# Block-sparse attention ahead of an FFN: scores in eight 64x32 tiles, probabilities turned by VectorE, block-diagonal values, sampled blocks copied on chip

## The chip, the cores and the metric

One core of a Trainium2 chip runs the whole program. Its engines are TensorE (PE; its weight loads are listed apart as PEld), VectorE (DVE), ScalarE (ACT), GpSimd (POOL) and SyncE (SP, which here only issues DMAs). Each engine works through its own instructions in order. The metric is the device time of one execution in microseconds (us); lower is better.

## The reference

Attention over a sparse set of key blocks, then a feed-forward net with an exact GELU. There are 4 batches, 8 heads, 768 positions and 64 dimensions per head. Positions form 24 blocks of 32. A query block sees its own block and both neighbours, the first and the last block, and three sampled blocks; the first and the last query block see all 24.

```python
scores = scale * np.matmul(q, k.transpose(0, 1, 3, 2))
mask = np.abs(blk_i - blk_j) <= window
mask = mask | (blk_i == 0) | (blk_j == 0) | (blk_i == n_blocks - 1) | (blk_j == n_blocks - 1)
for qb in range(n_blocks):
    for kb in sampled_blocks[qb]:
        mask[qb * block:(qb + 1) * block, kb * block:(kb + 1) * block] = True
scores = np.where(mask, scores, -1000000000.0)
scores = scores - np.max(scores, axis=-1, keepdims=True)
attn = np.exp(scores)
attn = attn / (np.sum(attn, axis=-1, keepdims=True) + 1e-09)
out = np.matmul(attn, v)
...
x = out.transpose(0, 2, 1, 3).reshape(B * S, H * D)      # 3072 x 512
h = x @ w_in                                             # 512 -> 2048
g = 0.5 * h * (1.0 + erf(h * inv_sqrt2))
return g @ w_out                                         # 2048 -> 512
```

A sampled block may repeat or coincide with a neighbour, the first or the last block; it must then count once.

## The kernel before

The work is cut into eight **units**: a batch and a half of its query blocks (12 blocks, 384 positions). A unit has an attention part and an FFN part. The main loop (L511) puts the FFN of one unit next to the attention of the next: first the eight steps of FFN1 (`ffn1_step`, L409), then `attention` (L432) of the next unit, into which the pieces of FFN2 (`ffn2_pieces`, L417; four matmuls each) are dealt as filler, one a round, to keep PE busy.

**Preparation.** Keys and queries come from HBM by DMA from POOL's queue, cast to bf16, with six consecutive positions in a partition. `prep_pair` (L187) turns a pair of heads on PE into the PSUM tile `pt` (two buffers of psT); DVE copies it to `kT` (L203), ACT scales it into `qT` (L205). For batches 1 to 3 this lies between the FFN1 steps of the second unit of the batch before.

**Attention by rounds.** A unit has two dense rounds (its one dense block, four heads each) and six sparse rounds (two query blocks each, the last one). A round has five stages:

- `stage_scores` (L296): 4 heads in 32-row strips; each query block meets its three neighbours straight from `kT` (96 columns) and 160 columns from `kg`, where the first, three sampled and the last key blocks stand side by side. Two row halves of PE (heads are paired in 64 partitions) and four column strips are used, so that the four products of a group stand in four tiles. DVE takes the row maxima (L319, one instruction per query block).
- `stage_exp` (L331): four ACT exponentials of 256 columns with the maximum as bias.
- `stage_transpose` (L342): PE turns the probabilities, 128x128 at a time, into PSUM tile `tp`; ACT copies it to `ps` (L351), every fourth time DVE (L353).
- `stage_av` (L356): products with the values, 65 columns (64 and a column of ones that gives the sum), from `vg0` (neighbours and first block) and `vg1` (sampled and last); then DVE adds 1e-9, takes the reciprocal and multiplies (L378 to L385).
- `stage_x` (L391): PE turns the outputs, DVE copies them into `xT` (L405), the input of FFN1.

`attention` runs these stages as a pipeline: in step `it` the scores of round it+1, the values of it-1, the transposes of it, the exponentials of it+1, the outputs of it-2, then one piece of FFN2.

**Gathers.** Sampled keys are copied on chip, with the block number in a register (`k_sampled`, L216, on DVE and POOL). Values go through a scratch copy in HBM (`v_scratch`, L223): each sampled block is fetched from there with its own DMA (`v_sampled`, L228, 33 a unit, on SP's and POOL's queues), the neighbours in larger ones (`v_fetch`, L252), and for batch 0 in part by DVE copies (`v_adjacent`, L233). `value_list` (L152) replaces a block number that would count twice by that of a block of zeros.

**Buffers.** psA (scores and FFN1 results) and psT have two buffers, psO (FFN2) and psV (value products) one each. In the head, the first score round runs after two pairs of heads are prepared.

## Time and profile before

| what | us |
|---|---|
| time, median of 3 runs | 362.96 |
| the three runs | 361.33, 362.96, 363.54 |
| span of the profiled execution (the page gives no other time for it) | 361.4 |
| first FFN1 step of the first unit starts | 52.0 |
| FFN1 of units 2, 4, 6 and 8 starts | 96.7, 181.1, 259.1, 334.9 |
| last FFN1, FFN2 and stores, to the end | 26.5 |
| busy: PE / PEld / DVE / ACT / POOL | 304.6 / 174.8 / 199.4 / 221.2 / 106.3 |

The groups of instructions that the change touches, of the whole run (busy time of the group; mean of one instruction):

| group | count | busy us | mean ns |
|---|---|---|---|
| PE score products, sparse (L301, two forms) | 1408 | 28.4 and 27.7 | 240 and 213 |
| PE transposes of probabilities (L347) | 448 | 46.9 | 233 |
| PE value products (L372, sparse) | 1408 | 25.4 | 203 |
| ACT exponentials of 256 columns (L337) | 176 | 69.6 | 480 |
| ACT copies of turned probabilities (L351) | 50 | 46.8 | 935 |
| DVE maxima of 512 columns (L319) | 88 | 57.1 | 686 |
| DVE copies of sampled keys (L220) | 149 | 20.0 | 224 |
| POOL copies of sampled keys (L220) | 115 | 27.7 | 299 |
| value DMAs from scratch, 32.5 KB each | 270 | | 4.3 to 5.0 us to landing |

How to read it: the busy time of a group is the time in which at least one of its instructions ran, and the mean is the length of one; where neighbours overlap, the mean is longer than the distance from one to the next. In the 40 slices of the span PE's clock is granted in full except in slices 4 to 6 (about 27 to 54 us), where it is halved. A busy PE is not a PE at its peak. What a stage costs is seen in the table by stretches of time and in the timeline, from where one start stands to the next.

### The profile page before, as it was taken

Reading aid. Unit: us, or ns where it says so; the run is one execution under the profiler, and the core shown is the slowest. Engines: PE = TensorE matmul, PEld = TensorE weight load, DVE = VectorE, ACT = ScalarE, POOL = GpSimd, SP = SyncE. Lnnn points to the kernel's source line nnn. Section 1 sums busy time; section 2 is a strip of 40 time slices with the busy share of each in tenths; the row PEclk is TensorE's granted clock in tenths of the full one; section 3 lists DMA queues with packets and bytes.
Section 4 is the critical chain, followed back from the end, with each engine's and each line's share of the span. In section 5 each row is a group of like instructions: output and inputs, shape, how many; then the busy total and the mean of one; then the engine's idle time right before and its main releaser. Section 6 shows DMA issues by size and latency. Waiting matters only on the chain.

```text
span 361.4 us, 13108 instructions
## 1 busy us (share of the span) xinstructions
PE 304.6 (84%) x5143; PEld 174.8 (48%) x5200; DVE 199.4 (55%) x606; ACT 221.2 (61%) x362; POOL 106.3 (29%) x248
## 2 busy tenths in 40 slices
PE   0852779958999979993999989998999999999994
PEld 0532545435554545452555555555554555455541
DVE  5598953698564854174546675157564862286000
ACT  1342754657658874683458875687558776786721
POOL 8393508600055505562302003863200310000000
PEclk9995558999999999998799999999999999999999
DMA  8988997992288999969377754959470630000001
GB/s 115 120 203 181 160 206 141 212 149 64 80 190 183 151 259 139 217 158 215 70 160 95 153 126 73 133 139 213 102 163 3 149 74 31 2 33 32 29 31 59
DMA packets 67328, 45.29 MB, mean 125 GB/s; under 512 B 30625, under 2 KB 61922, under 8 KB 67266
## 3 DMA queue, kind: packets, MB, share of 16 engines
q0 software_dynamic: 39104, 16.24, 38.1%
q1 hardware_dynamic: 28162, 28.21, 31.7%
q8 instruction: 41, 0.67, 0.8%
q14 instruction: 21, 0.17, 0.2%
HBM read 47.03 MB, written 9.62 MB: 157 GB/s over the span
## 4 chain that ended last, share of the span: by engine, by line
PE 53%; ACT 17%; DVE 14%; issue 9%; DMA 3%; POOL 2%; DVEq 0%; POOLq 0%; ACTq 0%
PE hp L413 25%; PE op L422 11%; ACT pp L337 9%; PE tp L347 6%; DVE nm L319 5%; PE sc L301 4%; PE av L372 4%; PE pt L193 4%; DVE vg L240 3%; ACT ps L351 3%; DVE nm L327 2%; DMA vg<-vscr 2%; ACT L339 2%; ACT pp L339 2%; POOL kg L220 1%
## 5 line engine op out<-in xcount | busy, mean ns | idle before, releaser
L413 PE MATMUL hp<-xT,w_in_sb 128*128 128x384 bf16 x512 | 90.5, 330 | 2.5 <-DVE xT L405 2.5
L422 PE MATMUL op<-w_out_sb,g 128*128 128x512 bf16 x327 | 85.6, 381 | 5.4 <-ACT os L427 1.4
L337 ACT ACTIVATE pp<-sc,nm 128x256 bf16<-128x256 f32 x176 | 69.6, 480 | 12.1 <-DVE den L378 7.2
L415 ACT ACTIVATE g<-hp 128x768 bf16<-128x768 f32 x64 | 51.9, 810 | 38.1 <-PE hp L413 38.0
L319 DVE TENSOR_REDUCE nm<-sc 128x2 f32<-128x512 f32 x88 | 57.1, 686 | 27.0 <-PE sc L301 19.1
L351 ACT COPY ps<-tp 128x1024 bf16<-128x1024 bf16 (+2 forms) x50 | 46.8, 935 | 38.6 <-PE tp L347 37.7
L413 PEld LDWEIGHTS <-w_in_sb 128*128 128x128 bf16 x512 | 48.5, 99 | 35.5 <-issue 5.0
L230 POOL DMA_DIRECT2D vg<-vscr x78 | 39.1, 503 | 78.6 <-DMA vscr<-vn 41.8
L422 PEld LDWEIGHTS <-g 128*128 128x128 bf16 x384 | 34.9, 98 | 34.2 <-issue 5.3
L347 PE MATMUL tp<-identity,pp 128*128 128x128 bf16 x448 | 46.9, 233 | 4.8 <-ACT pp L339 1.9
L327 DVE TENSOR_REDUCE nm<-sc 128x1 f32<-128x768 f32 x16 | 15.3, 958 | 53.7 <-PE sc L301 53.7
L372 PE MATMUL av<-vg,ps 128*32 128x65 bf16 x1408 | 25.4, 203 | 21.2 <-issue 7.8
L220 POOL COPY kg<-kT 128x128 bf16 x115 | 27.7, 299 | 50.6 <-PE sc L301 29.7
L372 PEld LDWEIGHTS <-ps 128*32 128x32 bf16 x1792 | 22.5, 99 | 37.0 <-issue 10.5
L301 PE MATMUL sc<-kT,qT 64*32 64x96 bf16 (+2 forms) x832 | 37.7, 234 | 3.1 <-issue 3.0
L301 PEld LDWEIGHTS <-qT 64*32 64x32 bf16 x1536 | 23.8, 96 | 33.3 <-issue 31.7
L347 PEld LDWEIGHTS <-pp 128*128 128x128 bf16 x448 | 27.5, 102 | 19.6 <-ACT pp L337 9.5
L109 POOL DMA_DIRECT2D vn<-in_v_dram x24 | 21.1, 916 | 42.7 <-DVE kg L220 41.9
L427 ACT COPY os<-op 128x512 f32<-128x512 f32 x24 | 14.2, 593 | 30.3 <-PE op L422 30.3
L301 PE MATMUL sc<-kg,qT 64*32 64x160 bf16 x704 | 28.4, 240 | 4.2 <-DVE kg L220 3.9
L203 DVE COPY kT<-pt 128x768 bf16<-128x768 bf16 x16 | 15.3, 957 | 16.0 <-PE pt L193 16.0
L385 DVE TENSOR_TENSOR xh<-av,rec 128x256 bf16<-128x256 f32 (+1 forms) x64 | 22.9, 358 | 2.2
(50 smaller groups left out, 228.8 us busy)
## 6 DMA issues: line engine op xcount, KB each, us to landing
vg<-vscr SPq DMA_DIRECT2D x192, 32.5 KB, 4.3
out_dram<-os SPq DMA_DIRECT2D x24, 256.0 KB, 2.1
vg<-vscr SPq DMA_DIRECT2D x6, 682.5 KB, 8.5
vscr<-vn SPq DMA_DIRECT2D x4, 780.0 KB, 4.1
kn<-in_k_dram POOLq DMA_DIRECT2D x8, 384.0 KB, 6.4
vn<-in_v_dram POOLq DMA_DIRECT2D x24, 128.0 KB, 7.2
vg<-vscr POOLq DMA_DIRECT2D x78, 32.5 KB, 5.0
vg<-vscr SPq DMA_DIRECT2D x6, 390.0 KB, 4.9
```

The lines of the kernel that those rows point to most:

```text
L220: copy(kg[:, (j - 1) % US, :, BL + BL * r:2 * BL + BL * r], kTs[b % 2][:, :, bass.ds(vals[j, r] * BL, BL)])
L230: engine.dma_start(out=vg1s[(j - 1) // US][BL * r:BL * r + BL, (j - 1) % US, :], in_=vscr[b][bass.ds(val * BL, BL), :])
L301: nc.tensor.matmul(out_, lhsT=qT[rows, h // 2, j * BL:(j + 1) * BL], rhs=rhs[rows], start=True, stop=True)
L319: nc.vector.tensor_reduce(out=nm[:, 2 * i:2 * i + 2], in_=A4[:, i], op=ALU.max, axis=AX.X, negate=True)
L337: nc.scalar.activation(pp[:, cols], A[:, cols], AF.Exp, bias=nm[:, i:i + 1])
L347: nc.tensor.transpose(T[:, c, :], pp[:, c * P:(c + 1) * P], identity)
L351: nc.scalar.copy(ps[:, 0:n, :], T[:, 0:n, :])
L372: nc.tensor.matmul(av[32 * hh:32 * hh + 32, s, :], lhsT=probs[:, 32 * hh:32 * hh + 32], rhs=vals[:, VW * h:VW * h + VW], start=(c == 0), s ...
L385: nc.vector.tensor_tensor(xh[:, at:at + n, :], av[:, 0:n, 0:D], rec[:, 0:n, None].to_broadcast([P, n, D]), op=ALU.mult)
L413: nc.tensor.matmul(hp[:, i, 0:UT], lhsT=w_in_sb[:, ki, (m + i) * P:(m + i + 1) * P], rhs=xT[:, ki, :], start=(ki == 0), stop=(ki == KIN - 1))
L415: nc.scalar.activation(g[:, m:m + 2, :], hp[:, :, 0:UT], AF.Gelu)
L422: nc.tensor.matmul(op, lhsT=g[:, m, t * P:(t + 1) * P], rhs=w_out_sb[:, m, :], start=(m == 0), stop=(m == KOUT - 1))
```

## The change

The units, the FFN and their interleaving stay. What changes:

- **Layout.** One tile `kvs[i]` holds, per key block, 128 columns of keys (four pairs of heads) and 2 x 130 columns of values. Values are block-diagonal: partitions 32hh to 32hh+31 hold 32 keys of head hh (of four), and heads 0 and 1 of a pair of strips have separate 65 columns, with zeros in the other's. The value DMAs (one a head, eight a batch) write there in place; `value_frame` writes the zeros and ones once. A 25th block has zero values and the keys of block 0. The scratch copy in HBM and all DMAs from it are gone.
- **Gathers.** For each query block three whole key and value blocks of 388 columns are copied on chip into `gbs`, with the block number (of `value_list`) in a register: 15 a batch by DVE, 51 by POOL, after the fourth FFN1 step of the batch before. In the head keys (128 columns) and values (260) are copied apart, as the keys of batch 0 lie in another tile, `k0`.
- **Scores.** Heads of the second group of four stand in the other row half, so that eight products (four heads, two groups) fall on eight 64x32 tiles. A query block has 24 products of 96, 64 and 96 columns instead of 16 of 96 and 160. One DVE instruction takes the maxima of a round.
- **Probabilities.** ACT writes the exponentials with the columns of two neighbouring key blocks interleaved, so that a pair of bf16 values fills a 4-byte word; one DVE instruction then turns all 32x32 blocks of words. The PE transposes and their copies are gone.
- **Values.** For two rounds (four query blocks) together: 64 rows (two heads' keys), 32 queries, 130 columns; eight tiles; 32 products a query block instead of 16. Division by DVE and output transposes once per two rounds; ACT copies to `xT` (two of them now).
- **Rounds.** Both dense blocks are in a batch's first unit: ten rounds there, six in the second. FFN2 pieces are single matmuls, 4 or 6 a round. psT has one buffer, psV is twice as large.
- **The head.** All eight preparations come first, then all ten rounds, without filler, then value copies on DVE, then all value products. Keys and queries are loaded whole, eight positions in a partition.

The diff, cut to its core:

```diff
+    V2 = 2 * VW
+    KC = NPR * BL
+    BW = KC + 2 * V2
+    PI = 8
+    PP = S // PI
...
+    kvs = [const.tile([P, NB + 1, BW], BF16, name=f"kv{i}") for i in range(2)]
+    gbs = [const.tile([P, US, NR, BW], BF16, name=f"gb{i}") for i in range(2)]
+    qT0 = const.tile([P, NPR, S], BF16, name="qT0")
+    qT1 = const.tile([P, (NB + 1) * KC], BF16, name="qT1")
+    qTs = [qT0, qT1[:, 0:NPR * S].rearrange("p (r s) -> p r s", r=NPR)]
+    k0 = qT1.rearrange("p (n c) -> p n c", c=KC)
+    kn = const.tile([P, H, PI * D], BF16, name="kn")
+    qn = const.tile([P, H, PI * D], BF16, name="qn")
+    ptd = const.tile([P, 2, NE, 2, BL, 2], BF16, name="ptd")
+    xTs = [const.tile([P, KIN, UT], BF16, name=f"xT{i}") for i in range(2)]
...
+    def load_v(b, h):
+        G, hh = divmod(h, 4)
+        c0 = KC + V2 * G + VW * (hh % 2)
+        nc.gpsimd.dma_start(out=kvs[b % 2][32 * hh:32 * hh + 32, 0:NB, c0:c0 + D],
+                            in_=v[b, h].rearrange("(n p) d -> p n d", p=BL))
...
+    def value_frame(i, engine):
+        kv = kvs[i]
+        engine.memset(kv[:, :, KC:BW], 0.0)
+        for hh in range(4):
+            c0 = KC + VW * (hh % 2) + D
+            engine.memset(kv[32 * hh:32 * hh + 32, 0:NB, c0:c0 + V2 + 1:V2], 1.0)
+
+    value_frame(0, nc.vector)
+    for h in range(H):
+        load_v(0, h)
...
+    def prep(b, which, pr, on_act):
+        src = kn if which == "k" else qn
+        pt = psT.tile([P, PI, PP], BF16, name="pt", tag="T")
+        for i in range(PI):
+                r = h2 ^ (pr // 2)
+                nc.tensor.transpose(pt[64 * r:64 * r + 64, i, :],
+                                    src[0:PP, 2 * pr + h2, i * D:(i + 1) * D],
+                                    identity[0:PP, 0:PP])
+            dst = keys(b)[:, 0:NB, BL * pr:BL * pr + BL].rearrange("q n (a i) -> q n a i", i=PI)
+            seen = pt.rearrange("q i (n a) -> q n a i", n=NB)
...
+    def gather(b, js, vals, engine, src=None, c0=0, c1=BW):
+        src = kvs[b % 2][:, :, c0:c1] if src is None else src
+            gb = gbs[(j - 1) // US]
+                engine.tensor_copy(gb[:, (j - 1) % US, r:r + 1, c0:c1],
+                                   src[:, bass.ds(vals[j, r], 1), :])
...
+    def rounds_of(hf):
+        js = list(range(j0, j0 + US))
+        dense = [("d", x, G) for x in (0, 1) for G in (0, 1)] if hf == 0 else []
+        return dense + [("s", tuple(js[i:i + 2])) for i in range(0, US, 2)]
...
+        def product(o, G, hh, j, rhs):
+            r = (hh % 2) ^ G
+            rows = slice(64 * r, 64 * r + 64)
+            pr = 2 * G + hh // 2
+            nc.tensor.matmul(o, lhsT=qT[rows, pr, BL * j:BL * j + BL],
+                             rhs=rhs[rows, :, BL * pr:BL * pr + BL], start=True, stop=True)
+        if rnd[0] == "s":
+            A4 = A.rearrange("p (g j c) -> p g j c", g=2, j=2)
+            for i, j in enumerate(rnd[1]):
+                gb = gbs[(j - 1) // US]
+                for c0, c1, rhs in ((0, 96, kT[:, j - 1:j + 2, :]),
+                                    (96, 160, kT[:, 0:NB:NB - 1, :]),
+                                    (160, 256, gb[:, (j - 1) % US, :, :])):
+                        for G in range(2):
+                            product(A4[32 * hh:32 * hh + 32, G, i, c0:c1], G, hh, j, rhs)
...
+            nc.vector.tensor_reduce(out=nm[:, 0:2 * n].rearrange("p (g j) -> p g j", g=2),
+                                    in_=A4[:, :, 0:n, :], op=ALU.max, axis=AX.X, negate=True)
...
+        def one(dst, src, bias):
+            nc.scalar.activation(dst.rearrange("p (c k e) -> p c e k", e=2, k=BL),
+                                 src.rearrange("p (c e k) -> p c e k", e=2, k=BL),
+                                 AF.Exp, bias=bias)
...
-        T = psT.tile([P, 8, P], BF16, name="tp", tag="T")
-        n = 4 * (len(grp) - 1) if grp[0] == "sparse" else NT
-        for c in range(n):
-            nc.tensor.transpose(T[:, c, :], pp[:, c * P:(c + 1) * P], identity)
-            nc.scalar.copy(ps[:, 0:n, :], T[:, 0:n, :])
-            nc.vector.tensor_copy(ps[:, 0:n, :], T[:, 0:n, :])
...
+    def turned(rnd):
+        pp = st.pop((rnd, "pp"))
+        if rnd[0] == "s":
+            w = 512 * len(rnd[1])
+            pt = ptpool.tile([P, 1024], BF16, name="pT")
+            nc.vector.transpose(pt[:, 0:w].bitcast(F32), pp[:, 0:w].bitcast(F32))
...
+            slots = [(rnd, i, j) for rnd in grp for i, j in enumerate(rnd[1])]
+            for G in range(2):
+                c0 = KC + V2 * G
+                for c in range(8):
+                    for s, (rnd, i, j) in enumerate(slots):
+                        x = len(rnd[1]) * G + i
+                        pv = st[rnd, "pt"][:, 256 * x:256 * x + 256]
+                        pv = pv.rearrange("p (c k e) -> p c k e", k=BL, e=2)
+                        if c < 3:
+                            src = kv[:, j - 1 + c, c0:c0 + V2]
+                        elif c < 5:
+                            blk = (0, NB - 1)[c - 3]
+                            blk = NB if abs(blk - j) <= 1 else blk
+                            src = kv[:, blk, c0:c0 + V2]
+                        else:
+                            src = gbs[hf][:, (j - 1) % US, c - 5, c0:c0 + V2]
+                        for h in range(2):
+                            rows = slice(64 * h, 64 * h + 64)
+                            nc.tensor.matmul(av[32 * s:32 * s + 32, h, V2 * G:V2 * G + V2],
+                                             lhsT=pv[rows, c // 2, :, c % 2], rhs=src[rows],
+                                             start=(c == 0), stop=(c == 7))
...
+            nc.scalar.copy(xTs[hf][:, :, t0:t0 + 32 * n], T[:, :, 0:32 * n])
...
+    def attention(b, hf, filler):
+        rounds = rounds_of(hf)
+        n = len(rounds)
+        ends = grouped(rounds, hf)
+        late = 12
+        per = -(-(KOUT * (UT // P) - late) // (n + 1))
+
+        def fill(m):
+            for _ in range(m):
+                next(filler, None)
         for it in range(-1, n + 2):
+            if it + 1 < n:
+                scores(b, rounds[it + 1])
             if 0 <= it - 1 < n:
+                turned(rounds[it - 1])
+            if it + 1 < n:
+                maxima(rounds[it + 1])
             if 0 <= it < n:
+                exponentials(rounds[it])
+            fill(per // 2 if it <= n - 1 else late // 4)
+            if it - 2 in ends:
+                outputs(hf, ends[it - 2])
+            if it - 1 in ends:
+                values(b, hf, ends[it - 1])
+                divided(ends[it - 1])
+            fill(per - per // 2 if it <= n - 1 else late // 4)
...
+        fetch()
+        groups = list(grouped(rounds, 0).values())
+        for i, grp in enumerate(groups):
+            values(0, 0, grp)
+            divided(grp)
+            if i:
+                outputs(0, groups[i - 1])
+        outputs(0, groups[-1])
...
+    for pr in range(NPR):
+        prep(0, "k", pr, False)
+    for pr in range(NPR):
+        prep(0, "q", pr, True)
+    spare_key(0, nc.vector)
+    gather_keys(J0[5:], v_pool0, nc.gpsimd)
+    gather_keys(J0[:5], v_dve, nc.vector)
+    for part in range(4):
+        load_w_in(part)
+    for part in range(2):
+    gather_values(J0[5:], v_pool0, nc.gpsimd)
+    gather_keys(J1, v_pool1, nc.gpsimd)
+    gather_values(J1, v_pool1, nc.gpsimd)
+    value_frame(1, nc.gpsimd)
+    first_attention(lambda: gather_values(J0[:5], v_dve, nc.vector))
...
+            if fresh:
+                prep(b + 1, "k" if s < 4 else "q", s % 4, s >= 4)
+                if s == 3:
+                    spare_key(b + 1, nc.vector)
+                    gather(b + 1, J0[:5], v_dve, nc.vector)
+                    gather(b + 1, J0[5:], v_pool0, nc.gpsimd)
+                    gather(b + 1, J1, v_pool1, nc.gpsimd)
```

509 lines of the change are left out of this document (160 added, 349 removed).

## The prediction

> **What bounds the kernel now.** I read the busy table by stage first. It was asked for from the second FFN1 step (batch 0, second half) on, two units with their FFN to a line; the next such step starts the next line:
>
> ```profile
> 96.60:181.00 84.40, 73.50 (x1272) 42.14 (x1288) 43.41 (x144) 55.03 (x91) 35.57 (x76) 0.96 0.90 176
> 181.00:259.00 78.00, 72.02 (x1272) 41.33 (x1288) 43.88 (x144) 54.97 (x91) 24.51 (x54) 1.00 0.76 135
> 259.00:334.80 75.80, 72.42 (x1272) 40.97 (x1288) 42.91 (x143) 54.91 (x91) 5.54 (x22) 1.00 0.25 61
> ```
>
> The columns are the stretch and its length, busy time of PE, weight loads, DVE, ACT and POOL, clock, DMA share and GB/s. The work is the same three times. PE is the bound at 72 to 73 us; the first two batches are 8.6 and 2.2 us longer than the third, with more DMA and hardly more PE work. The busy table of the last attention alone (310.0 to 334.7) has PE 23.2, ACT 18.6 and DVE 16.2 of 24.7 us. There the timeline shows ACT and PE in turn:
>
> ```profile
> 319.04 1.01 ACT L351 COPY ps<-tp 128x1024 bf16<-128x1024 bf16 x1 [0.38 <-PE tp L347]
> 319.95 1.57 ACT L337 ACTIVATE pp<-sc,nm 128x256 bf16<-128x256 f32 x4
> 320.35 0.43 PE L372 MATMUL av<-vg,ps 128*32 128x65 bf16 x32
> 320.72 1.14 PE L347 MATMUL tp<-identity,pp 128*128 128x128 bf16 x8
> 321.95 1.57 ACT L337 ACTIVATE pp<-sc,nm 128x256 bf16<-128x256 f32 x4 [0.43 <-PE tx L402]
> ```
>
> The transposes wait for the exponentials, and their 1.01 us copy out of PSUM stands on ACT between two rounds' exponentials: 2.6 us of ACT a round, in rounds of 2.5 to 3.1. The chain of waits holds one larger gap, in the middle of the value products:
>
> ```profile
> 166.04 0.35 PE av L372 x29
> 166.39 5.16 issue
> 171.55 0.25 PE av L372 x3
> ```
>
> What it waited for the profile doesn't name; it lies where sampled values come in by DMA.
>
> **The change, part by part.** First the loop, in the last batch's undisturbed times.
>
> *Removed.* A batch loses 112 PE transposes (56 ns start to start, 6.3 us, and waits of 0.2 to 0.3 us between pairs), 11.7 us of ACT copies (L351: 46.8 / 4), most of its value DMAs and POOL's issues of them.
>
> *Added on DVE.* Transposing 128x512 words has no row. Nearest are a 128x1024 bf16 copy out of PSUM at 0.68 and two 128x512 reduces at 1.29; I take 0.65 (ends 0.45 and 1.2: 3 us less, 10 us more over the kernel). One reduce of 1024 replaces two: 1.25, between 0.69 and 1.29. The division for two rounds is 0.16 + 0.18 + about 0.7 (128x256 took 0.42). The xT copies move to ACT, 0.59 each (row of 128x512, L351). A pair round then costs DVE 1.9 and half of 1.1, ACT 1.58 + 0.3 + 0.25 (os): both under 2.5. Exponentials written in interleaved pairs keep their 0.395 (upper end 0.59, L427's 512 columns: 9 us more in all).
>
> *PE.* Matmul starts in the records stand 3 to 4 ns apart inside a four of different tiles, and a four with 65 columns follows the last after 27 ns; eight tiles are therefore 54 ns, by issue and, at 130 columns, by streaming alike. So I take 0.06 us for eight value products (0.24 a block; now 0.19) and 0.15 a block for 24 scores (now 0.23). Where the shape of tiles changes, the next start comes 0.1 us late (scores to values 160 ns against 60, FFN2 to scores 309 against 216). The unit with six rounds, on PE: FFN2 48 x 0.216 = 10.4, scores 1.7, values 2.6, 12 output transposes 0.7, 27 changes of shape 2.7: 18.1. I took the instructions of PE, DVE and ACT in their order through these durations, each starting when its engine and its inputs are ready: PE waits 0.9 and 1.9 for os (one psO buffer, and os stands behind exponentials), 0.6 for the last division, and 0.9 pass until the last xT copy: 22.4. The unit with both dense blocks has 1.3 of dense scores and 1.5 of dense values more, 22.4 on PE, and waits of 4.4, the longest 1.0 for the last division, 0.7 for a transpose: 26.8. The same walk gives the old attention 28.5 where the trace has 24.7, as it lets a consumer start on whole tiles only; I take 1 us off each for that: **21.5 and 25.8**. FFN1 stays 10.9, and 15.4 with the preparations (8 pairs of 96 columns for 6 of 128). Their one psT buffer hides behind the 1.9 us steps: 0.96 copy, 0.6 transposes; without that cover, 0.5 for each of 8.
>
> *The gathers.* Between FFN1's fourth step and the attention DVE copies 15 blocks of 388 columns and POOL 51. POOL's 128 columns go every 0.24 us, and a 128-column memset took 0.12 more than a 1-column one; I take 0.5 for 388 (ends 0.24 and 0.72). Alone, DVE copied 11 blocks of 128 columns in 1.43; beside POOL's copies 6 took 2.98:
>
> ```profile
> 17.94 5.06 POOL L220 COPY kg<-kT 128x128 bf16 x21
> ...
> 19.83 2.98 DVE L220 COPY kg<-kT 128x128 bf16 x6
> ...
> 53.64 1.43 DVE L220 COPY kg<-kT 128x128 bf16 x11
> ```
>
> The first of the six lasted 1.83, the others came every 0.23, one to a POOL copy, and POOL's pace stayed. So here 15 x 0.5 = 7.5, from 8.8 after FFN1's start to 16.3, and the first maximum, due at 16.0, waits. PE has 2.5 us of queued scores and FFN2 as cover. I charge 0.7. [...]
>
> A batch is 25.8 + 21.5 + 10.9 + 15.4 + 0.7 = **74.3**, 1.5 under the clean 75.8; the larger gain is the 8.6 + 2.2 of the disturbed ones, as value DMAs leave the loop.
>
> *The head.* FFN1 starts at 52.0 now. The change (a) puts a 25x260 bf16 memset on DVE ahead of the block list: 3,250 words by 260 in 0.275 is 3.4 us, so the first kT copy comes at 11, not 9.1; (b) prepares all keys and queries through one psT buffer before any score: four times 0.96 + 1.05 + 0.1 and four times 0.81 + 1.05 + 0.1, so scores start at 27 (now 11.3); loads of 1.57 MB at the 121 GB/s of the first 10 us are in by 15; (c) runs ten rounds with DVE the bound: 1.9 to fill, 4 x 1.46, 5.5 x 1.9, ending at 45; (d) queues 15 value copies on DVE behind them and ahead of every division, beside a busy POOL: 6, ends 3 and 10; (e) then three groups of 2.0 (halved clock, as 27 to 54 us now) + 1.1, 0.8 for the dense one and 1.2 for the last outputs: FFN1 at **62** (57 to 69). POOL's queue holds key copies, six weight loads, then value copies for the second unit up to about 60, due at 75; and the next batch's loads behind them, due at 105.
>
> *Sum.* 62 + 12.8 (first FFN1 at a halved clock, 14.6 less the query halves) + 21.5 = 96.3, level with 96.6 now, since the early unit lost 28.4 us to value copies and holds one dense block less. 96.3 + 3 x 74.3 = 319.2; the last FFN1, FFN2 and stores take 26.6 as now: a span of 346. The profiled span is 361.4, within the runs' 361.3 to 363.5; the median lies 1.6 above it. That gives **348**.
>
> **The rivals.**
> *The forecast:* 335 to 359, chance 0.56.
> *Tiles that share columns don't run side by side* (slower). The eight tiles pair two row halves on one column strip; the trace has fours on four strips only, some with alternating row halves. If a strip takes its two in turn, eight values cost 0.12 and a block's scores 0.30: the walk gives 4.4 and 3.8 us more a unit, 28 in all: 376. It decides from about 0.09 for eight values, where the gain is gone. For it: no pair on one strip is to be seen. Against it: four tiles of both row halves start 3 to 4 ns apart. Chance 0.14.
> *Row halves that write one bank take turns.* The new scores write each of two banks from both row halves, the values keep a bank to each half. If that serializes, a block's scores cost 0.30, 0.3 and 1.2 us a unit, 6 in all: 354, chance 0.05. The old scores write one bank from both halves, in different partitions, and start 3 to 4 ns apart, which speaks against it. [...]
> *POOL keeps DVE out* (slower). If the first DVE gather waits seven POOL copies as at 19.83, 3.5 us more go to each of three units and the head: 359, chance 0.11. If DVE waits for all 51, the first maximum is 16 us late less 2 of cover, three times: 390, chance 0.05.
> *The head is later than the loop gives back:* single buffers, DVE's queue order and a cold clock make 70 of 62, with transposes at 1.2: 366, chance 0.09.
> *It doesn't do what it says:* if POOL can't keep up with the sampled blocks (0.72 a copy is 37 us of a 74 us batch, still under), PE waits on gathers instead of DMAs: no gain, 362. The copies are short against their cover, so the chance is within the two before.
>
> **How the numbers follow.** A measurement of this kernel tells about 1% from no change (3.6 us). Faster by over 1% are the forecast's 0.56 and the bank rule's 0.05; slower are the strips' 0.14, the starved DVE's 0.05 and most of the late head, 0.08; of the short lock (359) and the rest of the head 0.12 fall within 1%. Forecast 348. The range goes from 334 (transposes and tiles at their lower ends, 8 + 3 us, and no extra waits) to 374, which leaves out 390 and about half of the strips' case, as their unknown price is centred on 376. The likeliest case alone: 335 to 359.
>
> **What will show it.** Right: no transposes of probabilities on PE, ACT near 48 us a batch (17.8 + 13.5 in the attentions, 16 in FFN1), scores starting near 27, FFN1 near 62 and 96, batches of 74 to 75 without a 5 us gap; eights of tiles 50 to 60 ns apart; the DVE transpose at 0.65. Wrong: eights at 110 ns or more; maxima that wait for DVE gathers at the start of a batch; FFN1 past 70; PE waiting for POOL's copies in the second unit.

## The result: 12% slower, and where the profile has it

The changed kernel takes 408.0 us (median of four runs, 404.47 to 415.55) against 363.25 for the kernel before, a ratio of 1.120 (95% interval 1.114 to 1.127). The run of 415.55 fell in a slower state, at a lower granted clock, and the ratio leaves it out. The forecast was 348. The profiled execution's span is 405.8 against the 346 of the prediction's sum: 59.8 us to be found.

First the stretches from one second-unit FFN1 to the next, the view the prediction began with (stretch and length, busy time of PE, weight loads, DVE, ACT and POOL, clock, DMA share, GB/s), of the changed kernel:

```profile
120.16:205.10 84.94, 67.73 (x1721) 38.11 (x1739) 43.98 (x73) 50.41 (x87) 31.90 (x63) 0.96 0.61 49
205.10:298.12 93.02, 70.23 (x1720) 39.49 (x1738) 44.06 (x73) 50.71 (x87) 31.90 (x63) 0.91 0.57 45
298.12:379.11 80.99, 65.02 (x1721) 37.44 (x1739) 43.82 (x73) 50.47 (x87) 23.61 (x51) 1.00 0.06 22
```

The forecast was 74.3 each. The work did get less: in the last of them PE is busy for 65.0 of 81.0 us (72.4 of 75.8 before), ACT for 50.5 (54.9). What has grown is waiting. And the three stretches differ by more than before did, the longer ones with more DMA.

The first FFN1 starts at 82.7, not at 62. The timeline of the changed kernel's head (start, length, engine, line, work; in brackets the idle time before and what ended it) shows why:

```profile
42.19 11.52 POOL L201 COPY gb<-kv 128x260 bf16 x33
43.03 1.23 DVE L281 STREAM_TRANSPOSE pT<-pp 128x512 f32<-128x512 f32 x2 [0.45 <-ACT pp L264]
44.15 1.35 PE L299 MATMUL av<-kv,ptd 64*64 64x130 bf16 x41 [0.76 <-issue]
44.32 17.56 DVE L201 COPY gb<-kv 128x260 bf16 x15
53.66 5.50 POOL L124 MEMSET kv<- 128x6500 bf16 x1
...
61.57 0.31 DVE L336 TENSOR_SCALAR den<-av 128x4 f32<-128x4 f32 x1
...
62.63 0.74 PE L323 MATMUL av<-kv,pT 64*32 64x130 bf16 x40 [17.13 <-DVE xh L340]
```

DVE's 15 value copies take 17.56 us, not 6. The first lasted 14.93 and the second 5.95, overlapping: both were done at 59.3, when POOL's unbroken run of 33 copies and one memset ended. All divisions stand behind them, and PE has nothing to do for 17.1 us.

The loop's loss shows in the chain of waits. Two places of it, in batch 2's first attention and in batch 3's second one:

```profile
243.44 1.10 PE av L323 x67
244.54 2.29 issue
246.83 0.83 PE av L323 x57
...
250.35 0.68 PE av L323 x54
251.02 6.12 issue
257.14 1.00 PE av L323 x39
```

```profile
363.50 1.09 PE av L323 x114
364.59 1.31 issue
365.90 0.34 PE av L323 x13
```

"Issue" is the profile's word for a wait that it can't name; here PE stops in the middle of a group of value products, with no wait for an operand on record. The numbers of matmuls ahead of its stops, counted in the records from the program's start, are 735, 863, 2256, 2382, 2509, 4028, 4155, 4282 and so on: neighbours are 126 to 128 apart, and with a weight load to each that is every 256th instruction. The DMA records of the same trace show blocks of 16,384 bytes on queue 8: one from 253.75 to 255.56, inside the 6.12 us; PE goes on 1.6 us after it has landed. The page of the profile counts these blocks (packets, MB, share). Of before, and of the changed kernel:

```profile
q8 instruction: 41, 0.67, 0.8%
```

```profile
PE 280.7 (69%) x6889; PEld 161.2 (40%) x6952; DVE 196.6 (48%) x332; ACT 202.8 (50%) x344; POOL 146.5 (36%) x321
...
q8 instruction: 54, 0.88, 0.9%
```

(6,889 + 6,952) / 256 = 54.1 blocks; before, (5,143 + 5,200) / 256 = 40.4. So the suspicion is that PE waits for its own **code**: the steps of 256 instructions between its stops and the count of blocks agree. The 5.16 us gap of before, which the prediction laid to value DMAs, holds such a block too, from 168.79 to 170.17.

Of the new operations, most were sized well: eight tiles start 3 to 4 ns apart; a DVE transpose is 0.65 to 0.70; xT copies are 0.59. The one that moved is the exponential, in a round of four:

```profile
327.70 1.73 ACT L264 ACTIVATE pp<-sc,nm 128x256 bf16<-128x256 f32 x4 [0.54 <-DVE nm L252]
331.81 0.59 ACT L379 COPY os<-op 128x512 f32<-128x512 f32 x1 [2.39 <-PE op L374]
332.30 1.73 ACT L264 ACTIVATE pp<-sc,nm 128x256 bf16<-128x256 f32 x4
```

1.73 for four, where before had 1.57. The second line shows how a stop of PE spreads: the copy of FFN2's result waited 2.39 us for PE, and the exponentials stand behind it on ACT.

### The profile page after: what moved, and what is told of

Same layout as the page of the kernel before. It is cut to its first block, busy times and chain, and to the rows that moved or that the text cites. A ratio compares the mean times of both kernels' runs of the same rounds, so it can differ in the third digit from the quotient of the medians.

```text
span 405.8 us, 15457 instructions
## 1 busy us (share of the span) xinstructions
PE 280.7 (69%) x6889; PEld 161.2 (40%) x6952; DVE 196.6 (48%) x332; ACT 202.8 (50%) x344; POOL 146.5 (36%) x321
## 4 chain that ended last, share of the span: by engine, by line
PE 52%; DVE 18%; issue 15%; ACT 12%; DVEq 1%; ACTq 0%
PE hp L366 19%; PE op L374 13%; PE av L323 9%; ACT pp L264 7%; DVE gb L201 6%; PE sc L226 5%; PE pt L174 3%; DVE xh L340 3%; DVE nm L252 3%; ACT os L379 2%; ACT L264 2%; PE tx L350 2%; DVE nm L255 1%; PE av L299 1%; ACT xT L355 1%
## 5 line engine op out<-in xcount | busy, mean ns | idle before, releaser
L201 POOL COPY gb<-kv 128x388 bf16 (+1 forms) x204 | 88.6, 487 | 156.7 <-PE hp L366 101.5
L374 PE MATMUL op<-w_out_sb,g 128*128 128x512 bf16 x321 | 88.0, 384 | 19.6 <-ACT os L379 10.9
L264 ACT ACTIVATE pp<-sc,nm 128x256 bf16<-128x256 f32 (+1 forms) x192 | 92.6, 597 | 13.4 <-DVE nm L252 9.0
L252 DVE TENSOR_REDUCE nm<-sc 128x4 f32<-128x1024 f32 (+1 forms) x48 | 53.8, 1121 | 66.0 <-PE sc L226 65.3
L323 PEld LDWEIGHTS <-pT 64*32 64x32 bf16 x2816 | 29.0, 98 | 65.6 <-issue 42.9
L323 PE MATMUL av<-kv,pT 64*32 64x130 bf16 x1760 | 29.0, 239 | 37.1 <-DVE xh L340 18.8
L374 PEld LDWEIGHTS <-g 128*128 128x128 bf16 x384 | 31.3, 98 | 38.3 <-issue 11.4
L201 DVE COPY gb<-kv 128x388 bf16 (+1 forms) x60 | 39.1, 838 | 1.1 <-DVE kv L194 1.0
L281 DVE STREAM_TRANSPOSE pT<-pp 128x512 f32<-128x512 f32 (+1 forms) x48 | 30.8, 653 | 5.7 <-ACT pp L264 5.5
L226 PE MATMUL sc<-kv,qT 64*32 64x96 bf16 (+3 forms) x1152 | 23.1, 211 | 10.5 <-ACT pp L264 9.7
L92 POOL DMA_DIRECT2D kv<-in_v_dram x32 | 22.7, 716 | 20.4 <-DMA qn<-in_q_dram 13.4
L323 PE MATMUL av<-gb,pT 64*32 64x130 bf16 x1056 | 21.5, 241 | 9.4 <-issue 9.4
L226 PE MATMUL sc<-gb,qT 64*32 64x96 bf16 x704 | 22.8, 214 | 3.6 <-issue 3.6
L183 DVE COPY kv<-pt 128x768 bf16<-128x768 bf16 x12 | 11.5, 958 | 17.0 <-PE pt L174 17.0
## 6 DMA issues: line engine op xcount, KB each, us to landing
w_out_sb<-in_moe_w_out_dram POOLq DMA_DIRECT2D x2, 1024.0 KB, 18.1
```

The source lines that it names most:

```text
L92: nc.gpsimd.dma_start(out=kvs[b % 2][32 * hh:32 * hh + 32, 0:NB, c0:c0 + D], in_=v[b, h].rearrange("(n p) d -> p n d", p=BL))
L201: engine.tensor_copy(gb[:, (j - 1) % US, r:r + 1, c0:c1], src[:, bass.ds(vals[j, r], 1), :])
L226: nc.tensor.matmul(o, lhsT=qT[rows, pr, BL * j:BL * j + BL], rhs=rhs[rows, :, BL * pr:BL * pr + BL], start=True, stop=True)
L252: nc.vector.tensor_reduce(out=nm[:, 0:2 * n].rearrange("p (g j) -> p g j", g=2), in_=A4[:, :, 0:n, :], op=ALU.max, axis=AX.X, negate=True)
L264: nc.scalar.activation(dst.rearrange("p (c k e) -> p c e k", e=2, k=BL), src.rearrange("p (c e k) -> p c e k", e=2, k=BL), AF.Exp, bias=bias)
L281: nc.vector.transpose(pt[:, 0:w].bitcast(F32), pp[:, 0:w].bitcast(F32))
```

## The experiments

Theory L: in the head, POOL's run keeps DVE out. Theory F: PE waits for its code, and the loads for the next batch (2.3 MB, DMA share about 0.9) delay the fetch. Rivals: the waits are for data; for the exponentials; or, theory C, returns to FFN2 after small tiles are dearer than I had charged. Stage lengths below are taken from the first FFN1 matmul of a unit to its last, and from there to the next unit's first. In the changed kernel the attentions are 24.4, 33.5, 23.8, 40.8, 24.7, 31.3 and 24.6 (second and first units in turn), the FFN1 of first units 13.1, 13.1, 13.0 and 10.6.

### The head: e1_head

```diff
+    v_pool05 = block_numbers(J0[:5], POOL)
-    v_pool1 = block_numbers(J1, POOL)
...
+    gather_values(J0[:5], v_pool05, nc.gpsimd)
     gather_values(J0[5:], v_pool0, nc.gpsimd)
+    v_pool1 = block_numbers(J1, POOL)
...
-    first_attention(lambda: gather_values(J0[:5], v_dve, nc.vector))
+    first_attention(lambda: None)
```

> The 15 sampled value blocks that DVE copies in the head of the changed kernel go to POOL (ahead of its copies for the second unit); DVE copies none there. Theory L (POOL's unbroken run keeps DVE's first copy out for 15 us, and every division is queued behind it): the 17.4 us in which PE is idle before the first group's outputs (45.2 to 62.6) go, the first FFN1 starts at 65 if the two large PE gaps behind it stay, at about 60 if those shrink as the value products no longer meet the next batch's loads; time 385 to 391 from 408. Rival (the first division waits for something else, the value products or data that POOL brings until 59): FFN1 stays at 80 or later, time 403 or more.

Measured: 391.1 us (span 388.1), FFN1 at 58.4. The timeline of e1_head at the same place:

```profile
43.23 1.23 DVE L281 STREAM_TRANSPOSE pT<-pp 128x512 f32<-128x512 f32 x2 [0.45 <-ACT pp L264]
...
46.01 0.16 DVE L336 TENSOR_SCALAR den<-av 128x4 f32<-128x4 f32 x1 [1.55 <-PE av L299]
...
46.90 0.74 PE L323 MATMUL av<-kv,pT 64*32 64x130 bf16 x40 [0.93 <-DVE xh L340]
...
47.72 11.47 POOL L201 COPY gb<-kv 128x260 bf16 x33
```

The division follows the products at once, and so does the next one, at 49.20, beside the same run of POOL: DVE's divisions, which read PSUM (0.16 and 0.17 us for their first steps), and beside POOL's key copies its transposes (1.23 for two) weren't kept out, as its copies were. L stands. FFN1 came 24.2 us earlier, more than the lock: the value products of the head no longer meet the next batch's loads, and two gaps of 2.3 and 6.5 us at matmuls 735 and 863 shrink to 0.6 or less, with PE's program unchanged. But only 17 of the 24 us are gained. The loads now fall into the first attention of the loop, which grows from 24.4 to 30.4; its chain of waits has the same gap at another instruction:

```profile
80.61 0.83 PE av L323 x84
81.44 5.03 issue
86.47 0.84 PE av L323 x43
```

### Loads: e2_noload, e5_gate, e10_noloads

```diff
+                if b == 0:
-                for h in range(H):
-                    load_v(b + 1, h)
+                    for h in range(H):
+                        load_v(b + 1, h)
```

> The value loads of batches 2 and 3 are left out (those batches use the values of batches 0 and 1, so the output of the second half is not the reference's); every instruction on PE, DVE and ACT stays. Theory F (PE waits for its own code, which comes by DMA in blocks of 256 instructions, and the loads delay these fetches): the gaps stay at the same PE instructions, but the 2.6 and 6.3 us ones in batch 2's first attention and the 2.3 in batch 1's become 1.3 to 1.9; that attention goes from 40.8 to 31 to 32, batch 1's from 33.5 to about 31.5, the FFN1 stretches behind them from 13.1 to 10.6; together 16 us less, time 392. Rival (PE waits for gathered values or for POOL): the large gaps stay, time above 402. Under both, the last batch (attentions 31.3 and 24.6) does not move.

Measured: 400.0 us. Batch 2's first attention fell from 40.8 to 35.8 and the FFN1 behind it from 13.0 to 10.6; batch 1's attention stayed (33.5 to 34.6). Half of what F said: keys and queries were still loaded there, and a gap of 3.33 us (244.93 to 248.26) is left in batch 2.

```diff
+            if s == 0:
+                nv = [1] if u == 0 else [b + 2] if hf == 1 and b + 2 < B else []
+                nkq = [b + 1] if hf == 0 and b + 1 < B else []
+                if nv or nkq:
+                    nc.gpsimd.tensor_copy(hold, g[0:1, 0, 0:1])
...
```

> The head of e1_head, and POOL's loads for later batches held back by a one-element copy that waits for the first GELU of an FFN1: keys and queries of the next batch are loaded from the FFN1 of a batch's first unit on, values of the batch after next from the FFN1 of its second unit on (batch 1's all at the first FFN1). The same bytes at other times, and PE's program unchanged. If the loads cost what they do by delaying PE's code, the units that no longer meet them come to the last batch's lengths: the attention of batch 2's first unit from 42.9 in e1_head to 31.5 to 33, batch 1's from 33.8 to about 31.5, the FFN1 of first units from 13.3 and 12.2 to 10.6, the first attention of the loop from 30.4 to 25 to 28; time 370 to 376 against 391. Rival (the units' lengths come from their work and not from the loads): 386 or more.

(Left out are the same loads as before, of the batches in `nkq` and `nv`.) Measured: 394.9 us, no gain over e1_head. Batch 1's first attention did fall (33.8 to 30.9), but the first of the loop still met its loads (31.7), and batch 2's took 52.5. This last has another cause. The timeline of e5_gate there, POOL and DVE:

```profile
187.87 5.65 POOL L92 DMA_DIRECT2D kv<-in_v_dram  x8 [0.87 <-issue]
193.52 23.01 POOL L201 COPY gb<-kv 128x388 bf16 x51
```

```profile
192.18 26.16 DVE L201 COPY gb<-kv 128x388 bf16 x15
218.26 1.81 DVE L256 TENSOR_REDUCE nm<-sc 128x1 f32<-128x768 f32 x2
```

Theory L again, now in the loop. Eight DMA issues ahead of POOL's copies shifted these by some 1.3 us against DVE's. DVE's third copy started at 192.84 and lasted 22.85 us, to within 0.9 of the end of POOL's 51; then the rest came every 0.17 to 0.48. In the changed kernel itself the same two queues start within 0.3 us of each other and take turns, 0.48 us a copy. So there the two alternated, and here DVE was starved; what decides between them the runs don't show.

```diff
-            if b + 1 < B:
+            if False:
                 for hs in HALVES:
                     load_kq(kn, k, b + 1, hs)
```

> e1_head with all loads of keys, queries and values for batches 1 to 3 left out (these batches are computed from batch 0's keys and queries and from what stands in the value buffers, so the output is not the reference's). All that the loads cost PE goes: each first unit's attention 31.3, each second's 24.6, each FFN1 10.6 or 14.5, hence 81 a batch as in the last one, the first FFN1 at 58: a span of 363, a time of 365 against 391 for e1_head. If loads are not what lengthens batches 1 and 2 (84.9 and 93.0 against 81.0 in the changed kernel), the time stays above 380.

Measured: 368.1 us, span 365.0: 23.1 us less than e1_head. The three stretches are now alike:

```profile
96.20:176.30 80.10, 66.51 (x1720) 37.73 (x1738) 43.76 (x73) 50.38 (x86) 23.65 (x51) 0.98 0.07 23
176.30:258.50 82.20, 67.15 (x1720) 38.21 (x1738) 44.01 (x73) 50.73 (x87) 23.61 (x51) 0.96 0.06 22
258.50:338.30 79.80, 64.87 (x1721) 37.43 (x1739) 43.66 (x73) 50.51 (x87) 23.58 (x51) 1.00 0.06 23
```

This is the price of the loads as a whole. Part of it is the clock: in the changed kernel the FFN1 stretches at 168 and 260 us (13.1 and 13.0) ran at a granted clock of 0.81, behind stops of 2.08 and 6.12 us, the one of 10.56 at 1.00. From the end of the first FFN1 on, the granted clock was halved for 30.7 us in all in e1_head and for 10.2 in e10_noloads; how much of the 23.1 us that makes wasn't tried apart. But 80 is still not 74.

### Is it the code, where no loads run? e7_double, e12_fewer

```diff
-            for G in range(2):
+            for G in ((0, 1, 0, 1) if b == 3 else (0, 1)):
```

> In batch 3 alone each sparse value product is done twice (the second pass starts its sums anew, so the result is the same): 352 more matmuls and weight loads in each of the last two attentions, where no loads run. By issue alone (8.3 ns a pair) each grows by 2.9 us: 31.3 to 34.2 and 24.6 to 27.5. By theory F 704 instructions are 2.75 blocks of code more, each 1.1 us of issue and 1.5 to 1.8 us of waiting for the next: 7.0 to 8.0 us, to 38.3 to 39.3 and 31.6 to 32.6; time 422 to 424 against 414 by issue alone.

Measured: 431.4 us; the last two attentions 40.7 and 36.1, up 9.4 and 11.5. Issue alone (2.9) is out; it is more than F said too. The chain of waits of e7_double in the first of them:

```profile
327.22 0.93 PE av L323 x78
328.15 1.42 issue
329.57 1.27 PE av L323 x127
330.84 2.46 issue
333.30 0.66 PE av L323 x49
```

After 127 products with their loads, 1.27 us of work, comes the next stop, of 2.46; 128 products from 340.75 on take 1.27 again, with 2.46 of stop behind them. These bursts, longer than a block, stopped at block ends. Inside the value products of this attention the sum agrees with F: start to start they take 14.54 us for 6.58, which is 2.9 of issue and 5.0 of longer stops. In the last one they take 12.92 for 4.49, and a further stop of 1.66 us stands in the scores. What is left, some 1.5 us in each, isn't told apart; the granted clock was 0.92 and 0.95 there, for 1.00.

```diff
-                        for h in range(2):
-                            rows = slice(64 * h, 64 * h + 64)
-                            nc.tensor.matmul(av[32 * s:32 * s + 32, h, V2 * G:V2 * G + V2],
-                                             lhsT=pv[rows, c // 2, :, c % 2], rhs=src[rows],
-                                             start=(c == 0), stop=(c == 7))
+                        nc.tensor.matmul(av[32 * s:32 * s + 32, c % 2, V2 * G:V2 * G + V2],
+                                         lhsT=pv[:, c // 2, :, c % 2], rhs=src,
+                                         start=(c < 2), stop=(c > 5))
```

> e10_noloads with half as many instructions for the sparse value products: the two 64-row halves of a block's 128 keys are taken by one product of 128 rows, 176 matmuls and weight loads a unit in place of 352 (the output is not the reference's: sums run over four heads' rows). By columns streamed, 44 fours of 54 ns are 2.4 us for 2.9 by issue now. Everything else stays, the returns to FFN2 too. Theory F (the code fetch is what the attentions lack in units without loads): 352 instructions less are 1.4 blocks, each with 1.5 to 1.8 us of waiting, so some 2.9 us a unit go, 31 to 28 and 24.5 to 21.6, and the time falls from 368 to about 347. Theory C (the returns to FFN2 and the chain of exponentials set the units): at most 0.5 us a unit, 364.

Measured: 348.7 us, span 346.9, where F had 347 and C 364. The stretches of e12_fewer:

```profile
92.60:167.90 75.30, 66.49 (x1386) 36.35 (x1386) 43.75 (x73) 50.40 (x87) 23.58 (x51) 1.00 0.07 24
167.90:244.80 76.90, 68.05 (x1386) 36.39 (x1386) 43.86 (x73) 50.43 (x87) 23.54 (x51) 0.98 0.06 23
244.80:320.20 75.40, 66.46 (x1386) 36.17 (x1386) 43.75 (x73) 50.64 (x87) 23.52 (x51) 1.00 0.07 23
```

DVE, ACT and POOL do the same as in e10_noloads, PE is as busy, and each stretch is 4.4 to 5.3 us shorter. It isn't the products themselves. A group of four blocks takes 1.05 us from its first start to its last without a stop (e10_noloads, at 330.91) and 0.88 in e12_fewer (at 306.44): some 0.4 a unit, 3 of the 18.1 us. The stops can be counted in the records: from the head's value products on e10_noloads has 15 of 0.40 to 1.95 us that stand at block ends and end 1.2 to 1.6 us after a block has landed, 15.2 us in all, and e12_fewer has 4, 3.0 in all. So some 12 are stops. The last 3 aren't told apart; the clock is among them, halved for 10.2 us in e10_noloads and for 3.4 in e12_fewer. 11,088 instructions make 43.3 blocks, and the page has 43.

### Can another order hide it? e3_spread, e6_halves, e9_bunch

e3_spread deals five FFN2 matmuls into the middle of each group of value products, taken from before and after it:

```diff
             for G in range(2):
                 c0 = KC + V2 * G
+                if G:
+                    fill()
```

> The same PE instructions in another order: in the attentions of the loop some 5 of the FFN2 matmuls that were queued before and after each group of value products go into its middle, so that 256 instructions last 3 us in place of 1.1. Theory F: a fetch of 2.5 to 3 us is then mostly covered; the last batch's attentions go from 31.3 to about 27 and from 24.6 to about 22.5, in all 20 to 25 us less: time 383 to 388. Rival S (PE is slow by its own sequencer in small tiles and by changes of tile shape, 0.35 us each): two more changes a group cost 0.5 to 0.7 us, so the attentions stay or grow to 32.5 and 26, time 408 to 416.

Measured: 408.8 us, no gain (last attentions 33.1 and 24.7). In the last attention no stop in the middle of the products that ends with a fetch is left, so the burst was the cause of those; but its chain now runs through the other engines (from 361.87 to 363.63 through ACT's exponentials and its copy out of FFN2's buffer), with FFN2 missing where it had been the cover.

e6_halves puts half of each group's products into the next round (on e5_gate):

```diff
+            if it - 2 in split:
+                values(b, hf, ends[it - 2], (1,))
+                divided(ends[it - 2])
...
+            if it - 1 in split:
+                values(b, hf, ends[it - 1], (0,))
```

> e5_gate, and each group of value products of four blocks is cut in two halves (64 products each) that PE does in two successive rounds, next to the scores, so that no more changes of tile shape with FFN2 come in than now and 256 instructions never come in one burst. If the code fetch is what costs in units without loads too, the gaps of 1.5 to 1.8 us in the middle of the value products go: the last batch's attentions from 31.3 to 28 and from 24.6 to 23.2, in all some 15 us less than e5_gate, about 358. Rival (as in e3_spread other waits stand right behind: exponentials, the copy out of FFN2's one buffer): the attentions stay within 0.7 of 31.3 and 24.6, and the time within 5 us of e5_gate.

Measured: 403.6 us against 394.9; the last attentions 32.6 and 26.8. The large stop in the value products of the second is gone (0.6 is left), and in its place FFN2 stands still for 3.4 us between two of its own matmuls.

e9_bunch joins each round's FFN2 in one bunch:

```diff
-            fill(per // 2 if it <= n - 1 else late // 4)
+            fill(per if it <= n - 1 else late // 2)
...
-            fill(per - per // 2 if it <= n - 1 else late // 4)
```

> The changed kernel with the FFN2 matmuls of a round in one bunch ahead of the output transposes and the value products, in place of two halves around them: some 10 fewer returns to FFN2 in the attention of a first unit and 7 fewer in a second. Theory C (the first FFN2 matmul after small tiles starts 0.37 us after the last of them, 0.3 more than I had charged): my walk of the queues with that price gives 2.2 us less for first units and 0.3 less for second ones, whose waits for the last groups grow; 31.3 to 29.1 and 24.6 to 24.3 in the last batch, the time 400 to 403. Rival F (the code fetch alone sets these units): the value products now stand next to the scores in one longer burst, so the units keep their length or grow by 1 us: 408 to 414.

Measured: 417.5 us; last attentions 31.9 and 26.6. C falls: fewer returns to FFN2 brought nothing. And its price was misread. The page of the changed kernel has 321 matmuls of L374 where the program has 384; the first one after small tiles is the one whose record is missing (at 322.76 its weight load stands 139 ns after the last small start, and the first recorded matmul 370 ns after it). In e12_fewer, where every matmul is recorded, most such returns take 136 to 157 ns. Scores and value products now stand in one burst: the last batch's first attention has three stops of 1.4 to 1.6 us at block ends, two in value products and one in scores. In its second one PE waits 2.5 us for FFN2's buffer, and the FFN1 behind that wait runs at a clock of 0.86, 12.24 for 10.56.

### Smaller ones: e4_exp, e8_os, e11_best

```diff
-            nc.scalar.activation(dst.rearrange("p (c k e) -> p c e k", e=2, k=BL),
-                                 src.rearrange("p (c e k) -> p c e k", e=2, k=BL),
+            nc.scalar.activation(dst.rearrange("p (c k e) -> p c k e", e=2, k=BL),
+                                 src.rearrange("p (c e k) -> p c k e", e=2, k=BL),
```

> The exponentials walk their elements in the order in which they are written (contiguous writes, reads from PSUM interleaved by 32); the changed kernel walks them so that writes are interleaved in pairs. The result is the same. If the scattered write makes four exponentials last 1.72 us (before the change 1.58) and the dense one 1.11 (0.90), both return to 1.58 and 0.90, and the time falls by 2 to 4 us (404 to 406). Rival: the stride costs on either side, and they stay at 1.7 or grow; time 408 or more. The gaps of PE stay where they are under both.

Measured: 406.5 us, a difference that can't be told from none, but the groups answer (count, busy time, mean). Of the changed kernel, and of e4_exp:

```profile
L264 ACT ACTIVATE pp<-sc,nm 128x256 bf16<-128x256 f32 x176 | 75.4, 550 | 9.1 <-DVE nm L252 9.0
L264 ACT ACTIVATE pp<-sc,nm 128x768 bf16<-128x768 f32 x16 | 17.2, 1112 | 4.3 <-DVE nm L255 4.3
```

```profile
L264 ACT ACTIVATE pp<-sc,nm 128x256 bf16<-128x256 f32 x176 | 69.0, 482 | 11.2 <-DVE nm L252 10.7
L264 ACT ACTIVATE pp<-sc,nm 128x768 bf16<-128x768 f32 x16 | 14.1, 901 | 5.1 <-DVE nm L255 5.0
```

The interleaved writes cost 9.5 us of ACT; interleaved reads from PSUM cost nothing (482 ns, for 480 in the kernel before). ACT isn't the bound, so little of it shows.

```diff
-            nc.scalar.copy(os, op)
+            nc.vector.tensor_copy(os, op)
```

> The copy of FFN2's result out of PSUM (0.59 us, three a unit) goes from ACT, where it stands ahead of a round's exponentials and behind those of the round before, to DVE. If this order turns each late FFN2 into late exponentials (and these into late scores), the attentions get about 1 us shorter, 31.3 to 30.3 and 24.6 to 23.6, and the time falls to about 400. Rival (DVE's queue is as full: maxima and divisions come 0.6 us later for it): no change or up to 1 us longer a unit, 408 to 414.

Measured: 409.8 us, attentions 31.4 and 24.4: the rival's case. That FFN2's copy stands on ACT isn't what sets the units.

> e1_head, e4_exp and e9_bunch together (the result is the same as the reference's). If their gains add: 391 less 1.5 less 5 to 8, that is 381 to 385, still 5 to 6% above the kernel before. Rival: the freed waits fall together with the loads' fetch delays and it stays at 388 to 391.

Measured: 401.3 us, 10.2 more than e1_head: with the bunches it loses about what e9_bunch lost against the changed kernel (9.5). Of the kernels that compute everything, e1_head is the fastest changed one, and 7.7% slower than before (interval 6.6 to 8.7%). None beats the kernel before.

## Why the prediction was wrong, point by point

Two steps failed: (d) of the head, whose price was taken too low, and the loop's sum, which had no term for PE's code nor for the loads beside it. The span was to be 346 and was 405.8. By the spans of the profiled runs (repeats of a kernel differ by up to 4 us) the 59.8 us part as follows: the lock in the head, 17.7 (to 388.1, with what the moved loads gave back within it); the loads, 23.1 (to 365.0); and from there to 346.9, by taking instructions away, 18.1, of which some 12 are stops for code, 3 faster issue and 3 not told apart. 0.9 is left.

- **Step (d), the 15 value copies of the head: 6 us, measured 17.6.** The mechanism, DVE waiting for POOL, was in the prediction, with "ends 3 and 10". The prediction took the lock's length from one row (1.83 us, and turns afterwards) that happened to be the mild kind. Of the two rivals of a starved DVE, the one that waits for all of POOL's copies (chance 0.05) is what happened, but in the head, where it hadn't been priced. In the loop the gathers went as forecast: 0.48 a copy, the first dense maximum 0.7 to 0.9 us late (charged 0.7).
- **The loop, 74.3 a batch: measured 84.9, 93.0 and 81.0.** The list of what PE does had no term for its code. It went by time per instruction alone. A batch has 3,460 instructions on PE now and had 2,560 (matmuls and loads, in the tables by stretches), and a unit's 352 sparse products come in bursts of up to 128 with their loads, 1.2 us a block. Both sides of this were in the profile of before: 41 blocks on queue 8, and the 5.16 us gap. The prediction quoted that gap and read it as sampled values coming in by DMA; "the larger gain is the 8.6 + 2.2 of the disturbed" batches hung on this. As far as such stops were their cause, taking the value DMAs out wasn't enough: the next batch's loads stayed, and e10_noloads has them at 23.1 us. That such stops were the cause the trace of before bears out. Its chain of waits has these besides the 5.16:

```profile
127.54 1.22 issue
134.34 1.14 issue
211.62 1.25 issue
248.91 1.48 issue
```

All five end 1.3 to 1.6 us after a block of 16,384 bytes has landed (at 127.34, 134.05, 170.17, 211.55 and 248.81). That is 7.5 us in the first stretch and 2.7 in the second, against the 8.6 and 2.2; the third has none. Behind the 5.16 us gap the granted clock was also halved, from 168.68 to 175.51, which the section on time and profile before leaves out. No run took the loads out of the kernel before.
- **The rest of the walk held within some 2%.** With the loads, the lock and a fifth of PE's instructions away (e12_fewer), the span is 346.9: batches of 75.3, 76.9 and 75.4 for 74.3, the first unit 35.6 for 34.3 (12.8 + 21.5), the tail 26.7 for 26.6. The first FFN1 is at 57.0, but DVE has no value copies in that head, and without the 6 us of step (d) the prediction has 56, and a span of 340. That 346.9 meets the forecast's 346 is luck; that each error is small isn't. The attentions are 22.9 and 27.9 there on average, against walks of 22.4 and 26.8: the 1 us that the prediction took off each, because the old attention had come out too long, wasn't there. (In the unit with dense blocks the prediction's 22.4 on PE is 1.5 more than the terms that it lists, 18.1 + 1.3 + 1.5.)
- **Head by steps:** first kT copy at 12.0 (11), scores from 24.7 (27), rounds until 44.3 (45), and from there to FFN1 14.0 without the lock in e1_head and 12.5 in e12_fewer (11).
- **Sizes:** transposes 0.65 to 0.70 (0.65); eight value products 0.067 by issue, 8.3 ns a pair (0.054 to 0.06), 0.3 a unit; exponentials 0.43 (0.395, upper end 0.59); changes of shape 0.09 to 0.14 (0.1); xT copies 0.59 (0.59).
- **The other rivals:** tiles that share a column strip ran side by side: they start 3 to 4 ns apart, and the 48 scores of a round start within 0.37 us, 0.18 a block (0.15), where the strips' rival and that of the banks each had 0.30. So both are out. The head as such was 1 to 2.4 us late without step (d).
- The range's upper end, 374, was built from rivals about the new operations. Two of the three causes lie in what the change left alone: the loads, and the fetch of instructions.

In the head a DVE copy was out for longer than one instruction of POOL: 14.93 us, over 27 POOL copies of 0.40 each and a memset of 5.50. Nor does the trace show row halves taking turns at a bank: the scores write each bank from both halves, in different partitions, at the pace just given.

## What to carry to other kernels

Count an engine's instructions as well as their time: here PE stopped at the ends of blocks of 256 in bursts of short ones, for 0.40 to 1.95 us each in e10_noloads, and beside loads by DMA for up to 6.5 (changed kernel). A gap "by issue" in the middle of a group, with no operand to wait for, is to be counted in instructions from the program's start before it is laid to data. Never queue a DVE copy that something waits for beside an unbroken run of POOL's, without pricing the wait at the length of the whole run: it was 14.9 us in the changed kernel's head and 22.9 in e5_gate.

## What the runs showed of the hardware that I had not expected

- PE's code came by DMA in blocks of 16,384 bytes, 256 instructions (54 blocks for 13,841 instructions in the changed kernel, 41 for 10,343 before). In a kernel with hardly any load a block is 0.9 to 1.65 us on its way (median 1.05, e10_noloads), and PE goes on 1.2 to 1.6 us after it has landed, in the changed kernel 1.2 to 1.9. In bursts of tile products that made stops of up to 1.95 us (e10_noloads), and of 2.46 where the bursts are doubled (e7_double, 330.84 and 342.03). Beside a DMA share of 0.9 the fetch itself starts late in the two longest stops of the changed kernel, of 6.53 and 6.12 us: 2.73 us after PE has stopped (76.05 for 73.32, 253.75 for 251.02), where in its last batch it starts 0.68 to 1.23 ahead of the stop.
- In the later part of a group of 128 value products the records have one weight load and one small matmul every 8.3 ns (changed kernel, 371.99 to 372.77), though neighbours go to different tiles and start 3 to 4 ns apart elsewhere.
- DVE's copies from SBUF to SBUF beside a run of POOL copies took turns with them in the changed kernel's loop (0.48 us each), and one waited for the whole of the run or nearly so in its head (14.9 us) and in e5_gate (22.9). What decides wasn't settled.
- ACT paid for interleaved 2-byte writes (four exponentials 1.73 for 1.57), not for interleaved reads from PSUM (one 482 ns in e4_exp, 480 before).
- PE's granted clock in the changed kernel's loop was halved for 3.4, 6.8 or 10.2 us at a time, the longest from within the 6.12 us stop (255.15 to 265.39). FFN1 took 13.1 us at 0.81 and 10.56 at 1.00. What brings the clock down wasn't settled: stops of 2 us stand with and without it.
